# The last row group of a fused attention and gated-FFN kernel: its final 128 rows multiplied, copied and stored by column halves on two DMA queues

## The chip, the cores and the metric

The kernel runs on one core of one Trainium2 chip. The metric is device time in microseconds; lower is better. Executions of one kernel differ by up to 1.8 us here, which is more than the change was predicted to save. So the times are given, but the argument rests on the tails of the traces, one profiled execution of each kernel. There an undisturbed event recurs within some hundredths of a microsecond: the 384 KB store at the end landed after 2.31, 2.31 and 2.32 us in three traces.

## The reference

Four batches of q, k, v with N = 6016 rows and C = 256 columns go through attention over channels (a 256x256 matrix per batch), and the 24064 resulting rows go through a gated FFN (code abridged).

```python
def _attn_ref(q, k, v, tau):
    qn = q / (np.linalg.norm(q, axis=1, keepdims=True) + 1e-06)
    kn = k / (np.linalg.norm(k, axis=1, keepdims=True) + 1e-06)
    s = kn.transpose(0, 2, 1) @ qn / tau
    ...                                  # softmax over the last axis -> a
    return v @ a

def _moe_ref(x, w_gate, w_val, w_out):   # d_ff = 1536
    gate = 1.0 / (1.0 + np.exp(-(x @ w_gate)))
    return gate * (x @ w_val) @ w_out
```

## The kernel before

Rows are laid out so that each of 128 partitions holds 47 consecutive rows of a batch. They are handled in groups of four row tiles; the last group of a batch has three. For every group, `glu` makes the gated activations `hT` (twelve chunks of 128 of the 1536 hidden columns). `out_mms` then multiplies them, one group late, by `w_out`: twelve accumulating matmuls of 256 columns for each row tile. `flush` copies the PSUM tile into the group's SBUF tile, and the whole group is stored after its last row tile.

```python
    def out_mms(b, ci, n0, n1):
        t0, nt = groups[ci]
        hT = hts[b, ci]
        for n in range(n0, min(n1, nt * FC)):          # FC = 12
            s, f = divmod(n, FC)
            if n == 0:
                ffn[b, ci] = opool.tile([P, TPC, C], FP32, tag="osb", name="out_sb")
            if f == 0:
                ffn["ps"] = pso.tile([P, C], FP32, tag="o", name="ps_o")   # two PSUM buffers
            mm(ffn["ps"], hT[:, f, ds(s * P, P)], w_out_sb[:, f, :], f == 0, f == FC - 1)
            ...
    def flush():
        while pending:
            out_sb, s, ps, b, ci = pending.pop(0)
            t0, nt = groups[ci]
            nc.vector.tensor_copy(out=out_sb[:, s, :], in_=ps)
            if s == nt - 1:
                nc.sync.dma_start(out=out_rows[b][:, t0 : t0 + nt, :], in_=out_sb[:, :nt, :])
    # ... main loop over batches, groups and chunks cut ...
    for s in range(groups[NCH - 1][1]):                # the very last group: three row tiles
        out_mms(*prev, s * FC, (s + 1) * FC)
        flush()
```

## Time and profile before

| | before |
|---|---|
| median, 3 runs | 831.2 us (830.94 to 831.29) |
| span of the profiled run | 829.0 us |
| TensorE busy | 98% |
| last matmul's end to the end of the span | 3.7 us |

The page shows that TensorE bounds everything but the ends. The lines that carry this, the chain of waits in the tail, the store's landing and the DMA activity by narrow windows are all in the prediction below. A line of the chain is "start, duration, what". A line of the timeline is "start, duration, engine, line of the source, operation", where SPq and ACTq are the sequencers of the sync and scalar engines, whose durations are those of issuing a DMA. "Landing" is the time from the start of that issue to the completion semaphore.

I add up one stretch throughout and call it **the tail**: from the start of the first matmul of the last row tile to the end of the span. Its boundaries are taken from the single instruction and semaphore records of the trace, which are finer than the two decimals of the views. Before, it is 1.51 (matmuls, to the start of the last copy) + 0.43 (copy) + 0.03 (to the issue) + 2.31 (landing) + 0.92 (closing) = 5.19 us (the unrounded terms).

### The profile page before, as it was taken

The page shows a single profiled execution, that of the slowest core. Times are in us where ns is not written, and L with a number is a line of the kernel's source. Part 1 is how long each engine was busy: PE and PEld are TensorE (multiplying, and loading weights), DVE is VectorE, ACT ScalarE, POOL GpSimd, SP SyncE. Part 2 cuts the span into 40 slices and gives each one's busy share as a digit, 9 for nine tenths or more (in the row PEclk, how much of TensorE's full clock was granted, in tenths as well). Part 3 has the DMA queues.
Part 4 walks back from the last instruction along what each step waited for, and adds up shares of the span by engine and source line. Part 5 has one row for each costly group of instructions (what it writes and reads, how often), then busy time and mean ns, then how long its engine had stood idle before and what let it go on. Part 6 is the DMA issues. An engine that isn't in the chain of part 4 may idle for free.

```text
span 829.0 us, 13765 instructions
## 1 busy us (share of the span) xinstructions
PE 816.1 (98%) x5192; PEld 502.6 (61%) x5206; DVE 588.9 (71%) x1022; ACT 391.6 (47%) x644; POOL 83.1 (10%) x159
## 2 busy tenths in 40 slices
PE   7899999999999999999999999999999999999998
PEld 4556666665665666665575666666566566666666
DVE  6577777887667777778767777777766666666664
ACT  4654444446644444445654444444655444444442
POOL 5531100002120100000211010000000000000000
PEclk9999999999999999999999999999999999999999
DMA  9999623226946433223875352223323423322111
GB/s 209 207 206 207 113 52 86 57 60 131 159 87 124 96 85 60 57 52 84 156 140 126 81 105 59 51 63 75 64 62 63 72 52 87 67 48 73 43 36 71
DMA packets 78739, 77.17 MB, mean 93 GB/s; under 512 B 50769, under 2 KB 55633, under 8 KB 78673
## 3 DMA queue, kind: packets, MB, share of 16 engines
q0 software_dynamic: 23920, 38.81, 28.3%
q1 hardware_dynamic: 54608, 36.97, 17.6%
q8 instruction: 40, 0.66, 0.3%
q10 hardware_dynamic: 144, 0.52, 0.2%
q14 instruction: 27, 0.21, 0.1%
HBM read 78.64 MB, written 24.64 MB: 125 GB/s over the span
## 4 chain that ended last, share of the span: by engine, by line
PE 94%; DMA 4%; DVE 1%; issue 0%; POOL 0%; ACT 0%; POOLq 0%; ACTq 0%
PE ps_o L88 30%; PE ps_gate L88 29%; PE ps_val L88 29%; PE ps_s L88 4%; DMA q_sb<-in_q_dram 3%; PE ps_gh L88 2%; DMA w_val<-in_moe_w_val_dram 1%; DVE hT L423 0%; ACT g_sb L422 0%; DVE sq L176 0%; PE ps_n L88 0%; POOL k_sb L97 0%; POOL q_sb L97 0%; PE ps_tp L393 0%; DVE out_sb L449 0%
## 5 line engine op out<-in xcount | busy, mean ns | idle before, releaser
L423 DVE TENSOR_TENSOR hT<-ps_val,g_sb 128x512 bf16<-128x512 f32 (+1 forms) x576 | 391.2, 680 | 206.3 <-ACT g_sb L422 201.9
L422 ACT ACTIVATE g_sb<-ps_gate 128x512 bf16<-128x512 f32 (+1 forms) x576 | 338.1, 588 | 386.0 <-PE ps_gate L88 380.0
L88 PE MATMUL ps_gate<-vT,gh_G 128*128 128x512 bf16 (+1 forms) x1152 | 337.6, 375 | 0.6 <-ACT g_sb L422 0.4
L88 PE MATMUL ps_val<-vT,gh_H 128*128 128x512 bf16 (+1 forms) x1152 | 337.4, 375 | 0.4
L88 PE MATMUL ps_o<-w_out_sb,hT 128*128 128x256 bf16 x2256 | 326.2, 273 | 0.0
L88 PEld LDWEIGHTS <-hT 128*128 128x128 bf16 x2256 | 220.7, 98 | 124.8
L88 PEld LDWEIGHTS <-gh_H 128*128 128x128 bf16 x1152 | 112.7, 98 | 131.6 <-issue 1.4
L88 PEld LDWEIGHTS <-gh_G 128*128 128x128 bf16 x1152 | 112.4, 98 | 38.5 <-issue 0.6
L106 POOL DMA_DIRECT2D v_sb<-in_v_dram x48 | 25.6, 533 | 619.9 <-DMA vT<-v_sb 485.8
L449 DVE COPY out_sb<-ps_o 128x256 f32<-128x256 f32 x188 | 77.9, 414 | 13.5 <-PE ps_o L88 13.5
L88 PE MATMUL ps_s<-k_sb,q_sb 128*128 128x256 bf16 x376 | 66.0, 272 | 5.7 <-DMA k_sb<-in_k_dram 4.3
L88 PEld LDWEIGHTS <-q_sb 128*128 128x128 bf16 x376 | 36.6, 98 | 14.1 <-issue 6.3
L215 DVE TENSOR_TENSOR acc<-acc,sq 128x1024 bf16<-128x1024 bf16 (+1 forms) x66 | 44.2, 669 | 0.0
L176 DVE TENSOR_TENSOR sq<-q_sb 128x1024 bf16<-128x1024 bf16 (+2 forms) x44 | 29.4, 668 | 2.7 <-DMA q_sb<-in_q_dram 2.7
L97 POOL DMA_DIRECT2D k_sb<-in_k_dram x48 | 26.3, 549 | 16.5 <-DMA k_sb<-in_k_dram 8.9
L97 POOL DMA_DIRECT2D q_sb<-in_q_dram x48 | 26.2, 545 | 16.0 <-DMA q_sb<-in_q_dram 8.6
L176 DVE TENSOR_TENSOR sq<-k_sb 128x1024 bf16<-128x1024 bf16 (+2 forms) x34 | 22.4, 658 | 0.9 <-ACT sq L174 0.9
L376 ACT ACTIVATE gh_G<-ps_gh,rrow 128x512 bf16<-128x512 f32 x21 | 14.4, 687 | 12.7 <-PE ps_gh L88 8.8
L174 ACT ACTIVATE sq<-k_sb 128x1024 bf16<-128x1024 bf16 (+1 forms) x11 | 11.2, 1018 | 14.6 <-DMA k_sb<-in_k_dram 11.8
L88 PE MATMUL ps_busy<-ones_wide,ones_bf 128*128 128x512 bf16 x57 | 16.3, 412 | 1.7 <-DVE shift L127 1.6
L378 DVE TENSOR_SCALAR gh_H<-ps_gh,rrow 128x512 bf16<-128x512 f32 x22 | 16.4, 743 | 1.6 <-PE ps_gh L88 1.6
L472 DVE TENSOR_TENSOR acc<-acc,sq 128x1024 bf16<-128x1024 bf16 x16 | 11.1, 692 | 5.1 <-ACT sq L174 4.8
(65 smaller groups left out, 124.5 us busy)
## 6 DMA issues: line engine op xcount, KB each, us to landing
out_dram<-out_sb SPq DMA_DIRECT2D x44, 512.0 KB, 2.9
v_sb<-in_v_dram POOLq DMA_DIRECT2D x44, 256.0 KB, 3.8
q_sb<-in_q_dram POOLq DMA_DIRECT2D x43, 256.0 KB, 7.8
k_sb<-in_k_dram POOLq DMA_DIRECT2D x43, 256.0 KB, 8.5
out_dram<-out_sb SPq DMA_DIRECT2D x4, 384.0 KB, 2.5
w_gate<-in_moe_w_gate_dram POOLq DMA_DIRECT2D x3, 256.0 KB, 6.8
w_val<-in_moe_w_val_dram POOLq DMA_DIRECT2D x3, 256.0 KB, 7.4
w_out_sb<-in_moe_w_out_dram POOLq DMA_DIRECT2D x1, 768.0 KB, 12.6
```

The source lines that it names most:

```text
L88: nc.tensor.matmul(out, lhsT=lhsT, rhs=rhs, start=start, stop=stop, **kw)
L97: nc.gpsimd.dma_start(out=tl[:, :nt, :], in_=rows(src, b)[:, t0 : t0 + nt, :])
L106: nc.gpsimd.dma_start(out=v_sb[:, :nt, :], in_=rows(v, b)[:, t0 : t0 + nt, :])
L174: nc.scalar.activation(out=sq[:, :nt, :], in_=src[:, :nt, :], func=ACT.Square)
L176: engine.tensor_tensor(out=sq[:, :nt, :], in0=src[:, :nt, :], in1=src[:, :nt, :], op=ALU.mult)
L215: nc.vector.tensor_tensor(out=acc[:, :nt, :], in0=acc[:, :nt, :], in1=st[b]["sq", w][:, :nt, :], op=ALU.add)
L376: nc.scalar.activation(out=dst, in_=ps, func=ACT.Copy, scale=r)
L378: nc.vector.tensor_scalar(out=dst, in0=ps, scalar1=r, scalar2=None, op0=ALU.mult)
L422: nc.scalar.activation(out=g_sb[:, :n], in_=ps_gate[:, :n], func=ACT.Sigmoid)
L423: nc.vector.tensor_tensor(out=hts[b, ci][:, f, :n], in0=ps_val[:, :n], in1=g_sb[:, :n], op=ALU.mult)
L449: nc.vector.tensor_copy(out=out_sb[:, s, :], in_=ps)
L472: nc.vector.tensor_tensor(out=acc[w], in0=acc[w], in1=sq[w], op=ALU.add)
```

## The change

The intent is to shorten what follows the last matmul: the first two row tiles are stored early, and the last row tile is made in two halves of 128 columns, so that only a quarter-size copy and a small store remain at the end.

```diff
+    def last_rows(b, ci):
+        t0, nt = groups[ci]
+        s, half = nt - 1, C // 2
+        hT = hts[b, ci]
+        nc.sync.dma_start(out=out_rows[b][:, t0 : t0 + s, :], in_=ffn[b, ci][:, :s, :])
+        for n, queue in enumerate((nc.sync, nc.scalar)):
+            ps = pso.tile([P, half], FP32, tag="o", name="ps_end")
+            for f in range(FC):
+                mm(ps, hT[:, f, ds(s * P, P)], w_out_sb[:, f, ds(n * half, half)], f == 0, f == FC - 1)
+            end = opool.tile([P, half], FP32, tag=f"end{n}", name="end", bufs=1)
+            nc.vector.tensor_copy(out=end, in_=ps)
+            queue.dma_start(out=out_rows[b][:, t0 + s, ds(n * half, half)], in_=end)
...
-    for s in range(groups[NCH - 1][1]):
+    for s in range(groups[NCH - 1][1] - 1):
         out_mms(*prev, s * FC, (s + 1) * FC)
         flush()
+    last_rows(*prev)
```

## The prediction

> **What bounds the kernel now.** I read the busy table and the chain of the page first, because they say whether a change in the last few microseconds can matter at all.
>
> ```profile
> span 829.0 us, 13765 instructions
> PE 816.1 (98%) x5192; PEld 502.6 (61%) x5206; DVE 588.9 (71%) x1022; ACT 391.6 (47%) x644; POOL 83.1 (10%) x159
> PE 94%; DMA 4%; DVE 1%; issue 0%; POOL 0%; ACT 0%; POOLq 0%; ACTq 0%
> ```
>
> TensorE is busy for 98% of the span and carries 94% of the chain. The change touches none of that: it edits only what comes after the last gate and value matmuls. So the whole question is the tail, from the last row tile's 12 output matmuls to the end of the program. I read the chain of waits there, then the timeline of the sync queue, then a table of narrow windows with DMA share and GB/s in the last two columns.
>
> ```profile
> 820.96 4.38 PE ps_o L88 x40
> 825.34 0.02 issue
> 825.36 0.42 DVE out_sb L449
> ```
> ```profile
> 825.82 0.33 SPq L451 DMA_DIRECT2D out_dram<-out_sb  x1
> ```
> ```profile
> 826.40:826.60 0.20, 0.00 (x0) 0.00 (x0) 0.00 (x0) 0.00 (x0) 0.00 (x0) 1.00 0.00 0
> 826.60:826.80 0.20, 0.00 (x0) 0.00 (x0) 0.00 (x0) 0.00 (x0) 0.00 (x0) 1.00 0.90 353
> ...
> 827.40:827.60 0.20, 0.00 (x0) 0.00 (x0) 0.00 (x0) 0.00 (x0) 0.00 (x0) 0.56 0.89 353
> 827.60:827.80 0.20, 0.00 (x0) 0.00 (x0) 0.00 (x0) 0.00 (x0) 0.00 (x0) 0.50 0.19 62
> 827.80:828.00 0.20, 0.00 (x0) 0.00 (x0) 0.00 (x0) 0.00 (x0) 0.00 (x0) 0.50 0.00 0
> ```
> ```profile
> out_dram<-out_sb SPq DMA_DIRECT2D x1, 512.0 KB, 2.6
> out_dram<-out_sb SPq DMA_DIRECT2D x1, 384.0 KB, 2.3
> ```
>
> The exposed tail is thus a serial sum. TensorE ends at 825.34. The last copy runs 825.36 to 825.78. The store of the whole group (384 KB, three row tiles) is issued at 825.82. No byte moves for 0.8 us; then the engines move data from about 826.6 to 827.65. The store lands 2.3 us after its issue, near 828.12, and the span ends 0.9 us later at 829.0. Altogether 3.66 us after the last matmul. Two thirds of the bytes in that last store were ready long before: the copy of the second row tile ended at 824.47.
>
> **What the Trainium skill says.** The page "DMA: Bandwidth & Descriptors", section "Anatomy of one DMA", gives a transfer as a fixed part of about 2.0 us plus bytes at 436 GB/s, the fixed part being mostly the write receipt (fitted on the GpSimd path). The trace agrees on the slope: the last two stores differ by 128 KB and 0.3 us, so 131 KB / 0.3 us = 437 GB/s. It has a smaller fixed part: 2.3 us less 393 KB / 437 GB/s = 0.9 us leaves 1.4 us. The same page, section "Issuing engines are not separate DMA queues", says that several issuing engines save only the sequencer's time to issue; here that is 0.33 us (row above). The page "TensorE: Matmul & The Clock Gate", section "Back-to-back issue gap", gives two figures for 128 columns: about 56 ns for a matmul by itself and about 81 ns in a stream in which each has its weight load. The trace can decide, as it has such streams:
>
> ```profile
> 35.83 0.61 PE L393 MATMUL ps_tp<-ident_bf,v_sb 128*128 128x128 bf16 x8
> 30.32 0.54 PE L88 MATMUL ps_n<-ones_bf,sq 128*128 128x1 bf16 x16
> ```
>
> The eight transposes each load new 128x128 weights and stream 128 columns. One of them is 219 ns by itself, so seven gaps take 0.61 - 0.22 = 0.39 us, or 56 ns each. The sixteen one-column matmuls with a fresh weight load each (163 ns by itself) leave (0.54 - 0.163) / 15 = 25 ns per pair. So the weight loads, although each is recorded as 98 ns, overlap and can follow each other every 25 ns. I go by the trace and use 56 ns.
>
> **The change part by part.**
> *Matmuls.* Twelve matmuls of 256 columns go, at 4.38 / 40 = 0.1095 us each, 1.31 us together. Twenty-four of 128 columns come, with twelve more weight loads. At 56 ns that is 1.34 us: +0.03 us on the path. The order of instructions shows that the first matmul of each half waits for a DVE semaphore, as it takes over a PSUM buffer. For the second half that is the copy of the second row tile, ended at 824.47. The last row tile starts at 825.34 - 1.31 = 824.03, its first half ends near 824.70, so the second half finds its buffer free with 0.2 us to spare.
> *Copies.* One copy of 128x256 goes (0.42 us), two of 128x128 come. The first runs under the second half's matmuls. The second is on the path. Its cost I take from the column slope of the vector engine on PSUM sources:
>
> ```profile
> L423 DVE TENSOR_TENSOR hT<-ps_val,g_sb 128x512 bf16<-128x512 f32 x528 | 364.5, 691 | 182.3 <-ACT g_sb L422 180.5 <-PE ps_gate L88 0.4 <-PE ps_val L88 0.2
> L423 DVE TENSOR_TENSOR hT<-ps_val,g_sb 128x384 bf16<-128x384 f32 x48 | 26.7, 556 | 24.1 <-ACT g_sb L422 21.4 <-PE ps_gh L88 2.2
> ```
>
> 128 columns fewer save 691 - 556 = 135 ns, so the copy becomes 0.42 - 0.135 = 0.28 us: -0.13 us on the path.
> *Stores.* The 384 KB store becomes 256 KB issued on the sync queue at about 824.51, 64 KB on the same queue at about 825.04 (824.70 + 0.02 + 0.28 + 0.04), and 64 KB on the scalar queue at the end. The first should land 2.0 us after issue (2.3 less 0.3), at 826.5; the second at about 826.7. Neither is last. The last store has 320 KB fewer than before, at 437 GB/s 0.75 us less, so 1.55 us to landing. But its runs in DRAM are 512 B instead of 3 KB and its bytes are few; I add 0.1 us for packets that are less efficient, an estimate that no view here supports closely. So 1.65 us: -0.65 us.
> *Two queues.* The sync sequencer would finish the issue of the first half at 825.04 + 0.33 = 825.37, before the second half's copy ends (825.67). The second queue takes away a wait that is not there: 0.
> *Everything before 824 us.* The new tiles come after all others in the last SBUF pool, and the instruction order of every engine is unchanged up to there: 0.
>
> Sum: last copy ends 825.37 + 0.02 + 0.28 = 825.67, issue at 825.71, landing 825.71 + 1.65 = 827.36, against 828.12: 0.76 us earlier. With the same 0.9 us after it, 831.2 - 0.76 = 830.4 us.
>
> **Rivals.**
> First, **weight loads bind the half-width matmuls.** At 81 ns (the page's stream) the twenty-four take 1.94 us, +0.63 instead of +0.03, and the change would yield 0.15 us: 831.0. At the recorded 98 ns per load it would be 2.35 us, +1.04, and the kernel would lose 0.3 us: 831.5. The gaps of 56 and 25 ns in the trace speak against both.
> Second, **the landing time of a small store is nearly all fixed.** If a 64 KB store in 512 B runs takes about 2 us to land (the page's fixed part), the gain is 0.3 + 0.13 - 0.03 = 0.4 us: 830.8. For it: 0.8 us pass before the first byte and about 0.5 us after the last whatever the size. Against it: the measured 2.3 us leaves only 1.4 us of fixed part.
> Third, **the two queues collide.** The 256 KB store and the two halves use the same DMA engines. The first occupies them from about 825.3 to 826.0, the second a little after, the third not before 826.5. They hardly meet; for a collision to cost anything the first would have to start half a microsecond late.
> Fourth, **the closing 0.9 us grows,** since the program now ends with one more store and queue to be waited for. These are semaphore waits of 17 to 28 ns each in the trace, so at most 0.1 us.
>
> **Range and chances.** My mean is 830.4. The mechanisms spread it from 829.9 (nothing added for small packets and a still shorter fixed part) to 831.0 (the first rival at 81 ns, or the second with a longer closing). The three runs of before spread over 0.35 us, which is comparable with the gain. I take 829.9 to 831.1 for 8 in 10. Two per cent is 16.6 us, over four times the whole exposed tail of 3.66 us; so faster by 2% is out of reach, and slower by 2% would need something that the diff doesn't contain. Within 2%: 0.99.
>
> **What would show it.** In the changed profile: (1) the 24 half-width matmuls span about 1.34 us plus one latency, with gaps of 56 ns (81 or 98 tells the first rival); (2) the two small copies last about 280 ns, the first beginning about 0.67 us before the second; (3) the scalar queue's store lands 1.55 to 1.75 us after issue (2.0 tells the second rival); (4) the 256 KB store has stopped moving data before the last store starts; (5) about 0.9 us from the last landing to the end, and a span near 828.2. The prediction would be wrong if the half-width stream ran at the rate of its weight loads, if the small store took as long to land as the large one, or if the time of the long middle moved by more than some tenths of a microsecond for a reason outside the diff.

## The result, and the profile after

| | before | after |
|---|---|---|
| median | 831.21 us (6 runs, 830.94 to 831.69) | 830.59 us (6 runs, 830.48 to 831.27) |
| ratio | 1 | 0.9993 (95%: 0.998 to 1.0006) |

A ratio here is the mean time of one kernel's runs over that of the other's of the same rounds, so not quite the ratio of the medians. The medians differ by 0.62 us, and the interval includes no change.

The profiled run of the changed kernel happens to be its slowest, 831.27 us with a span of 829.2, which is longer than the 829.0 of before. The chain of waits early on points to why. First before, then after:

```profile
30.51 6.79 DMA w_val<-in_moe_w_val_dram
37.30 0.04 issue
37.34 0.59 PE ps_gh L88 x2
```
```profile
32.60 8.11 DMA w_val<-in_moe_w_val_dram
40.71 0.04 issue
40.75 0.59 PE ps_gh L88 x2
```

The weights landed at 40.71 instead of 37.30 us in this execution, while the pipeline started up. Numbered from the start, the two kernels' matmuls are 0.10 us apart at number 240 (40 us) and 0.63 us apart at number 260 (44 us), and stay 0.63 us apart up to number 4800 (766 us). No edit of the change lies there, and the delay belongs to this execution: one_queue (below), whose program differs from the changed one only in the queue of one store at the end, starts its last row tile at 823.84 us, where before started it at 823.85 and this run at 824.48. So the two spans can't be compared; the tails can. The timeline of the changed kernel's tail:

```profile
824.48 1.51 PE L88 MATMUL ps_end<-w_out_sb,hT 128*128 128x128 bf16 x24
824.68 0.42 DVE L449 COPY out_sb<-ps_o 128x256 f32<-128x256 f32 x1 [0.89 <-PE ps_o L88]
825.14 0.33 SPq L458 DMA_DIRECT2D out_dram<-out_sb  x1
825.36 0.29 DVE L464 COPY end<-ps_end 128x128 f32<-128x128 f32 x1 [0.25 <-PE ps_end L88]
825.67 0.64 SPq L465 DMA_DIRECT2D out_dram<-end  x1
826.03 0.29 DVE L464 COPY end<-ps_end 128x128 f32<-128x128 f32 x1 [0.39 <-PE ps_end L88]
826.35 0.35 ACTq L465 DMA_DIRECT2D out_dram<-end  x1
```

Its DMA view of the last 6 us, sizes and landings:

```profile
out_dram<-out_sb SPq DMA_DIRECT2D x1, 256.0 KB, 2.3
out_dram<-end SPq DMA_DIRECT2D x1, 64.0 KB, 1.9
out_dram<-end ACTq DMA_DIRECT2D x1, 64.0 KB, 1.6
```

The reader sees the intended order: the store of two row tiles while TensorE works, the first half's copy and store behind it, and only the last 64 KB store at the end. Term by term, in us:

| term of the tail | before | after | difference | predicted |
|---|---|---|---|---|
| first matmul to last copy | 1.51 | 1.55 | +0.04 | +0.03 |
| last copy | 0.43 | 0.29 | -0.13 | -0.13 |
| copy's end to issue | 0.03 | 0.03 | 0.00 | 0 |
| last store, issue to landing | 2.31 | 1.57 | -0.74 | -0.65 |
| last landing to end ("closing") | 0.92 | 1.29 | **+0.37** | 0, at most 0.1 |
| sum | 5.19 | 4.72 | -0.47 | -0.76 |

Two things in this profile were not in the prediction: the closing grew by 0.37 us, and the issue of the first half took 0.64 us, where every one of the 48 output stores of before took 0.33 to 0.35.

### The profile page after: what moved, and what is told of

It reads as the page before. It is cut to its first block, busy times and chain, and to the rows that moved or that the text cites. A ratio compares the mean times of both kernels' runs of the same rounds, so it can differ in the third digit from the quotient of the medians.

```text
span 829.2 us, 13794 instructions
## 1 busy us (share of the span) xinstructions
PE 816.6 (98%) x5204; PEld 502.9 (61%) x5218; DVE 588.7 (71%) x1023; ACT 391.6 (47%) x644; POOL 83.0 (10%) x159
## 4 chain that ended last, share of the span: by engine, by line
PE 94%; DMA 4%; DVE 1%; issue 0%; POOL 0%; ACT 0%; POOLq 0%; ACTq 0%
PE ps_o L88 30%; PE ps_gate L88 29%; PE ps_val L88 29%; PE ps_s L88 4%; DMA k_sb<-in_k_dram 3%; PE ps_gh L88 2%; DMA w_val<-in_moe_w_val_dram 1%; DVE hT L423 0%; ACT g_sb L422 0%; DVE sq L176 0%; PE ps_end L88 0%; POOL q_sb L97 0%; PE ps_n L88 0%; POOL w_gate L139 0%; POOL k_sb L97 0%
```

## The experiments

**Theories.** For the closing: after its last store the sync engine waits, in a fixed order and one by one, for eight completion semaphores that the DMAs of the sync and scalar queues take in turn. The order of instructions shows that the last store takes the eighth before and the second after; the six behind it are then paid for after it lands. Rival: it is slower because the last store now sits on a second queue, the scalar one. The view of the closing line in the few tenths after the last landing shows what is at stake. Before:

```profile
L619 SPq DRAIN  x2: 7/10/13, 828.2 to 828.3; - x2
L619 SPq EVENT_SEMAPHORE  x1: 28/28/28, 828.1 to 828.1; - x1
```

After:

```profile
L634 SPq EVENT_SEMAPHORE  x7: 28/28/28, 827.9 to 828.3; - x7
L634 SPq DRAIN  x2: 7/10/13, 828.4 to 828.4; - x2
```

One semaphore instruction on the sync sequencer after the last landing before, seven after. Their starts are 0.06 us apart, and six of them make 0.37 us.

For the slow issue: in the tail of the changed kernel, and not in that of before, there is a DMA of one 16 KB packet on a queue of kind "instruction". Before and after, from the pages:

```profile
q8 instruction: 40, 0.66, 0.3%
```
```profile
q8 instruction: 41, 0.67, 0.3%
```

Such a packet comes about every 20 us through the whole run, in which TensorE runs some 260 of its 10,407 instructions. The change adds 24 TensorE instructions, and one more fetch falls due, at 824.97 to 825.93 us, just ahead of the stores. Rival: a store issued half a microsecond behind another on the same queue is slow in any case.

Two edits serve several experiments. "Tiny loads" turn the semaphores' round by n places, in the middle of the run, where the sync queue has time:

```diff
+    turn = [consts.tile([16, P], FP32, name=f"turn{i}") for i in range(n)]
...
             block = b + 1 < B and ci in (9, 10)
+            if (b, ci) == (1, 5):
+                for tl in turn:
+                    nc.sync.dma_start(out=tl, in_=q[0][:16, :P])
```

"Tiny matmuls" move TensorE's instruction fetches ahead by 60 instructions, in an idle stretch at the start:

```diff
     busy(9)
+    ps_tiny = psv.tile([P, CH], FP32, tag="v", name="ps_tiny")
+    for _ in range(30):
+        mm(ps_tiny[:, :1], ones_bf, ones_wide[:, :1], True, True)
```

All kernels gave correct results. Those of one call shared their runs of the kernel before (medians 831.05 and 831.07 us, 9 runs each).

### before_lane0: the kernel before, its last store on the first semaphore

Edit: tiny loads with n = 1, nothing else.

> The kernel before, with one extra tiny load (16x128 fp32) on the sync queue in the middle of the run, so that the last store takes the first of the eight completion semaphores instead of the eighth. Theory (the closing walks the eight semaphores in a fixed order, 0.06 us each, and those behind the last store's are paid after it lands): the time from the last landing to the end of the span grows from 0.92 to about 1.35 us, all else in the tail as in the kernel before, so the time grows by about 0.4 us. Rival (the closing grew because a store ended on the scalar queue): 0.92 us stays, as here the last store is on the sync queue; time unchanged within noise.

Measured: 831.65 us (831.42 to 831.72, 5 runs; ratio 1.0006, 0.9992 to 1.002). Tail 5.62 us, of which matmuls, copy and landing are those of before to 0.01 us and the closing is 1.35. The closing line's view after the last landing:

```profile
L624 SPq EVENT_SEMAPHORE  x8: 27/28/28, 828.1 to 828.5; - x8
L624 SPq DRAIN  x2: 7/10/13, 828.6 to 828.7; - x2
```

Eight instead of one, and 0.43 us more, with no store on the scalar queue. The theory's number came out; the rival's did not.

### after_lane7: the changed kernel, its last store on the eighth semaphore

Edit: tiny loads with n = 6.

> The changed kernel, with six such tiny loads in the middle, so that the last store (still on the scalar queue) takes the eighth semaphore. Theory: last landing to end falls from 1.29 to about 0.92 us, and the time from the first matmul of the last row tile to the end from 4.56 to about 4.19 us; about 0.4 us faster than the changed kernel, 0.8 faster than before. Rival (scalar queue): the closing stays at 1.29 us.

Measured: 830.3 us (829.94 to 831.76, 5 runs; ratio 0.9993, 0.998 to 1.0006). The closing fell to 0.90 us, with the last store still on the scalar queue; so the queue isn't the cause. After the last landing the sync engine's sequencer has one semaphore instruction, not seven:

```profile
L639 SPq EVENT_SEMAPHORE  x1: 28/28/28, 829.1 to 829.1; - x1
```

The profile is that of the slowest of the five runs (831.76 us): it starts its last row tile at 825.50 us, 1.0 us later than the changed kernel's, and only its tail is used. The tail is 4.48 us instead of the expected 4.19, however. The matmuls take 1.55, the copy 0.29, and the last store lands after 1.70 us instead of 1.57. The store is issued 0.03 us after the copy, as before. So 0.13 us of the miss is in that landing, and 0.16 in my expectation: it started from 4.56 us, a total counted from the chain, which shows the first matmul later than its own record does; counted as in the tables, that is 4.72. The timeline shows the second disturbance, worse than in the profile after:

```profile
826.69 0.93 SPq L467 DMA_DIRECT2D out_dram<-end  x1
```

And the DMA view of its last 6 us has the fetch and the late landing:

```profile
q8 instruction: 1, 0.02, 1.2%
...
out_dram<-end ACTq DMA_DIRECT2D x1, 64.0 KB, 1.7
```

The instruction fetch here took 1.13 us, to 827.24. One of the sixteen completions of the 256 KB store came at 828.75 us; the other fifteen came by 828.17. The data of the first half's store then moved from 828.12 to 828.50 us and overlapped with those of the last store (828.31 to 828.71); undisturbed they are apart, as in after_lane7_shift below (to 826.38, and from 826.57). That fits the later landing, but no run separates it from the fetch itself.

### one_queue: both halves on the sync queue

```diff
-        for n, queue in enumerate((nc.sync, nc.scalar)):
+        for n, queue in enumerate((nc.sync, nc.sync)):
```

> The changed kernel, with both halves stored from the sync queue. The prediction says that the second queue is worth nothing: the last store's issue starts within 0.05 us of the copy's end, as with two queues, unless the first half's issue takes 0.64 us again as in the profile after, when it may start up to 0.05 us late. Theory of the semaphore order: closing stays at 1.29 us (the last store is still on the second of the eight). Rival (scalar queue): closing falls to 0.92 us. A third view, that two queues matter: landing of the last store later by 0.3 us or more.

Measured: 830.58 us (830.45 to 831.03, 5 runs; ratio 0.9995, 0.9982 to 1.0007). Tail 4.93 us. The closing is 1.28: the rival about the scalar queue fails once more, as no store is on it here. But my expectation on the queues failed too: the issue of the first half took 0.80 us, the last issue began 0.25 us after its copy's end instead of 0.03, and the tail is 0.21 us longer than with two queues. Here the second queue does save something, because the sync sequencer is held up.

### whole_own_store: the store split alone

```diff
-        for n, queue in enumerate((nc.sync, nc.scalar)):
-            ...                                    # two halves of 128 columns
+        ps = pso.tile([P, C], FP32, tag="o", name="ps_end")
+        for f in range(FC):
+            mm(ps, hT[:, f, ds(s * P, P)], w_out_sb[:, f, :], f == 0, f == FC - 1)
+        end = opool.tile([P, C], FP32, tag="end0", name="end", bufs=1)
+        nc.vector.tensor_copy(out=end, in_=ps)
+        nc.scalar.dma_start(out=out_rows[b][:, t0 + s, :], in_=end)
```

with tiny loads, n = 7.

> Only the store is split: the last row tile keeps its twelve 256-column matmuls and one 128x256 copy, but has a store of its own (128 KB, 1 KB runs) on the scalar queue; seven tiny loads put the last store on the eighth semaphore. From the first matmul of the last tile to the end: 1.31 + 0.02 + 0.42 + 0.04 + landing 1.7 + closing 0.92 = 4.41 us, against 5.02 before and 4.19 expected of the halves with the same semaphore. If small stores' landing is nearly all fixed, the landing is under 1.6 us and the halves gain only by their copy.

Measured: 830.47 us (830.34 to 831.98, 5 runs; ratio 0.9995, 0.9982 to 1.0008). Tail 4.71 us: matmuls 1.51, copy 0.43, landing 1.72, closing 1.02. The landing is 0.59 us shorter than that of 384 KB, so it goes by size. The expectation counted from the chain again; with the first matmul's record it would have been 4.59, and 0.10 of the remaining 0.12 us are in the closing: one semaphore instruction after the landing as intended, but one sync drain took 0.13 us. What delayed that drain stays open. No instruction fetch fell into this tail (40 on the page), as the matmul count is that of before.

### one_queue_shift: one queue, the instruction fetch moved away

Edit: one_queue plus the tiny matmuls.

> Both halves stored from the sync queue, as in one_queue, plus thirty one-column matmuls (sixty TensorE instructions) in TensorE's idle time at the start, which move every later instruction fetch of TensorE ahead by sixty instructions, some 2.5 us in the tail. Theory (the 16 KB instruction fetch that falls into the tail occupies one DMA engine, and the sync queue's issue of the first half stretches until 0.38 us after that fetch ends): the issue of the first half takes 0.33 us instead of 0.80, the last store is issued 0.04 us after its copy instead of 0.25, and first matmul of the last tile to the end is 4.72 us instead of 4.93. Rival (a store issued half a microsecond behind another on the same queue is slow in any case): the issue still takes 0.6 to 0.9 us and the tail stays at 4.93.

Measured: 830.58 us (830.46 to 830.65, 4 runs; ratio 0.9995, 0.9979 to 1.001). The last fetch now starts at 821.1 us, 3.3 us earlier than in one_queue (some 2.5 had been expected). Both issues of halves took 0.33 us. The timeline merges them; without the fetch, then with it (one_queue):

```profile
825.20 1.01 SPq L465 DMA_DIRECT2D out_dram<-end  x2
```
```profile
825.03 1.28 SPq L465 DMA_DIRECT2D out_dram<-end  x2
```

The last store is issued 0.03 us after its copy, and the tail is 4.68 us, within 0.04 of what was expected. The rival (two stores close together on one queue are slow in any case) fails: the same two stores, 0.54 us apart as before, are not slow. Nor is a fetch enough by itself: in the kernel before, four of the 48 stores were issued while one was under way (at 158.8, 405.3, 440.7 and 541.1 us), with no other store close ahead, and each took 0.34 us; in the tails with a fetch, the 256 KB store was issued during it and took 0.33. What was slow in all three is a store issued behind another while the fetch was under way. In the three runs that have fetch and stretched issue, the issue ends 0.38 us after the fetch does (825.93 and 826.31 in the kernel after, 827.24 and 827.62 in after_lane7, 825.45 and 825.83 in one_queue). By which path the fetch holds up the issue, these runs don't show.

### after_lane7_shift: both disturbances taken away

Edit: after_lane7 plus the tiny matmuls.

> after_lane7 with the same thirty one-column matmuls at the start. Theory: no fetch between the last tile's matmuls and the end; all sixteen completions of the 256 KB store within 0.2 us (in after_lane7 one of them came 0.58 us behind the rest); issue of the first half 0.33 us; the last store lands 1.57 us after its issue instead of 1.70; first matmul of the last tile to the end 4.35 us instead of 4.48. Rival: straggler and long issue stay.

Measured: 830.01 us (829.95 to 830.01, 5 runs; ratio 0.9987, 0.9975 to 1.0). The tail is 4.33 us: 1.55 matmuls, 0.29 copy, 0.03, 1.55 landing, 0.90 closing. All sixteen completions of the 256 KB store came within 0.19 us. Its timeline, to be held against that of the changed kernel:

```profile
825.03 0.33 SPq L467 DMA_DIRECT2D out_dram<-end  x1
825.39 0.29 DVE L466 COPY end<-ps_end 128x128 f32<-128x128 f32 x1 [0.39 <-PE ps_end L88]
825.71 0.35 ACTq L467 DMA_DIRECT2D out_dram<-end  x1
```

The first half's issue is back at 0.33 us, and the last copy begins as soon after its matmuls as before. The tail is 0.39 us shorter than the changed kernel's and 0.86 us shorter than that of before, and the time is 1.06 us below the median of before in the same rounds. The upper end of the interval is 1.0.

### uneven_lane7_shift: 192 and 64 columns

```diff
-        for n, queue in enumerate((nc.sync, nc.scalar)):
+        for n, (c0, cn, queue) in enumerate(((0, 192, nc.sync), (192, 64, nc.scalar))):
```

with widths and offsets `cn` and `c0`, both kinds of tiny work kept.

> The same with the last tile's columns split 192 and 64 instead of 128 and 128. If the copy goes by 1.05 ns a column and the store by its bytes, the last copy takes 0.22 us instead of 0.29 and the last store lands 0.07 us sooner: 4.2 us from first matmul to end, the best version. If runs of 256 B cost more than their bytes, the landing stays at 1.57 or grows and the gain is at most the copy's 0.07 us.

Measured: 829.96 us (829.87 to 830.54, 5 runs; ratio 0.9988, 0.9976 to 1.0001). The last copy took 0.225 us, as expected, but the 32 KB store in runs of 256 B landed after 1.59 us, where 64 KB in runs of 512 B took 1.55. The tail is 4.30 us: the copy's 0.07 us, less the store's 0.03. Size, run length and spacing changed together: the data of this last store (826.55 to 826.85 us) also overlapped with those of the 96 KB store ahead of it (to 826.73), so what kept the landing from falling is not shown. This split gained only the copy's part, and the two versions can't be told apart by time.

### halves_one_store: matmuls and copies split, one store

```diff
+            nc.vector.tensor_copy(out=ffn[b, ci][:, s, ds(n * half, half)], in_=ps)
+        nc.sync.dma_start(out=out_rows[b][:, t0 : t0 + nt, :], in_=ffn[b, ci][:, :nt, :])
```

in place of `end` and the three stores.

> Only matmuls and copies are split: two halves of 128 columns, both copied into the group's tile, and one store of 384 KB as before (eighth semaphore). From the prediction's terms +0.05 us (matmuls) and -0.13 us (copy): 5.11 us from first matmul to end against 5.19 before; landing 2.3 us and closing 0.92 us as before. If weight loads bound the halves, +0.6 us or more.

Measured: 831.0 us (830.83 to 832.67, 4 runs; ratio 1.0004, 0.999 to 1.0018). Tail 5.08 us, closing 0.90, landing 2.32. The fetch is there too, from 824.45 to 825.51, but this store's issue begins only at 825.79, after the fetch, and takes 0.33 us. Halving alone is thus worth 0.11 us in the tail (0.10 by its matmuls and copy alone); the rest of the gain is the store's.

## Why the prediction was right or wrong

The time was inside the range (830.59 us against 829.9 to 831.1), and "within 2%" was right. The prediction of 830.4 took 0.8 us off; the medians show 0.62 and the tails 0.47. The range was wide enough to hide a miss of 0.37 us in one term, so the time alone confirms little, and that it came nearer to the prediction than the tails do is within the noise. Point by point:

- **TensorE bounds the middle and the change leaves it alone**: right. The 0.63 us between the two profiled runs arose in the start-up, where no edit lies.
- **Half-width matmuls at 56 ns, not 81 or 98**: right. In the changed kernel the starts of consecutive ones are 55 or 56 ns apart, and 65 once, at the change of PSUM buffer. The first rival is out. halves_one_store agrees: its stretch to the last copy is 1.55 us.
- **Copy 0.28 us**: right (0.29).
- **Landing 1.65 us**: right within 0.1 (1.57). Undisturbed it was 1.55 (after_lane7_shift), which is the size's share without the 0.1 us added for short runs. The second rival (about 2 us, nearly all fixed) is out for 64 KB. In tails without a fetch the landing fell from 1.72 us at 128 KB to 1.55 at 64 KB, and no further at 32 KB (1.59).
- **No collision between the stores**: right for the last store, which in the profile after began to move data 0.86 us after its issue, against 0.83 before. In after_lane7, with the fetch in the way, their data did overlap.
- **"with the same 0.9 us after it", and "at most 0.1 us" in the fourth rival**: wrong, and this is the step that failed. It was 1.29 us, so sign (5) failed too. I had the durations of the closing's semaphore waits (17 to 28 ns) but multiplied by too few, and didn't ask their order: they start 0.06 us apart, and six of them stood behind the last store's. before_lane0 and after_lane7 show it from both sides, 0.43 us added to a kernel with the old tail and 0.39 us taken from the new. Over all ten traces the closing was 0.90 to 0.92 us with the last store on the eighth semaphore (1.02 in whole_own_store, with the late drain), 1.28 to 1.29 on the second and 1.35 on the first.
- **"The second queue takes away a wait that is not there: 0"**: wrong for this kernel, right for the tail without the instruction fetch. With the fetch, one queue cost 0.21 us; without it the last issue followed its copy at once on one queue too. The step that failed is the issue time of 0.33 us: it was taken from stores with no other store close ahead, and didn't hold behind one during a fetch (0.64 to 0.93 us).

With the closing put in, the prediction's sum gives 0.39 us and the measured tail 0.47; the difference is the landing, which was 0.08 us better than assumed.

## What to carry to other kernels

At the end of a kernel the gain of a smaller last store is its landing time, and what follows the landing must be read too: how many completion semaphores this program still walked through after the last store landed depended on which of them that store took, and it cost 0.37 us, almost half of the gain. A change that adds instructions can also move an instruction fetch into a stretch that was free of it. A difference of half a microsecond in 830 is better taken from the tails of the traces than from a handful of times, as the start-up alone shifted one whole run by 0.6 us here.

## What the Trainium skill lacked or had wrong

- "TensorE: Matmul & The Clock Gate", section "Back-to-back issue gap": gives about 81 ns for a sustained stream of 128-column matmuls with weight loads. Here a stream of 24 such pairs ran 55 to 56 ns apart, the page's figure for a matmul by itself; pairs of 64 columns (uneven_lane7_shift) ran 28 to 30 ns apart, and pairs of one column 25.
- "Runtime: NRT & Kernel Launch", section "Instruction fetch mechanics": says that instructions come in blocks of 16 KiB and that crossing a boundary costs one tail-bump of a DMA, "mostly hidden". The traces agree on the block (packets of 16384 B about every 20 us, with some 260 TensorE instructions between them). What it lacks is that each took 0.9 to 2.0 us of DMA time, and that in three tails a store issued behind another during the fetch took 0.64 to 0.93 us to issue instead of 0.33; in one of them a completion came 0.58 us behind the rest.
- "DMA: Bandwidth & Descriptors", section "Anatomy of one DMA": a fixed 2.0 us plus bytes at 436 GB/s, fitted on the GpSimd path. Stores from the sync and scalar queues landed in 2.31 us for 384 KB, 2.03 for 256 KB, 1.72 for 128 KB and 1.55 for 64 KB in tails without a fetch: the slope holds (435 GB/s between 64 and 384 KB), the fixed part is about 1.4 us.
- Same page, section "Issuing engines are not separate DMA queues": says that a second issuing engine saves only the sequencer's issue time, usually small relative to the DMA. That held in kind, but the time was not always the 0.33 us of a store by itself: in one_queue the first half's issue took 0.80 us, and the last store began 0.25 us after its copy instead of 0.03.
- No page says that the closing of a program walks the completion semaphores of the DMAs in a fixed order, 0.06 us each, so that the last store's place in their round matters: 0.90 us to 1.35 us here.
